# Local-and-global attention before a feed-forward layer: the softmax laid out by quarters of 32 queries with their global keys in the same 128 columns

## The chip, the cores and the metric

The kernel runs on one core of a Trainium2 chip. The metric is the time of one execution on the device in microseconds (us). The kernel before took 942.32 us, the median of 3 runs (941.04 to 943.88). TensorE is called PE here, VectorE DVE, ScalarE ACT, GpSimd POOL; SP is the engine whose queue issues nearly all transfers.

## The reference

```python
B, H, Sl, D = 8, 8, 512, 64;  Sg = 32;  window = 32;  scale = 1 / sqrt(D)
k_all, v_all = concat([k_g, k_l]), concat([v_g, v_l])         # along the keys
out_g = softmax(scale * q_g @ k_all.T) @ v_all                # 32 global queries see all 544 keys
s_ll  = where(abs(i - j) <= window, scale * q_l @ k_l.T, -1e9)  # local: a band of 65 keys
s_l   = concat([scale * q_l @ k_g.T, s_ll])                   # and the 32 global keys
out_l = softmax(s_l) @ v_all
x = concat([out_g, out_l], axis=2), heads side by side        # 4352 rows of 512
h = x @ w_in                                                  # 512 -> 2048
y = where(h > 0, h, exp(min(h, 0)) - 1) @ w_out               # 2048 -> 512
```

All inputs are fp32 but the two weight matrices, which are float64. The output is fp32.

## The kernel before

The program has two parts that run interleaved: attention, which makes x, and the feed-forward part, which takes x in blocks of 256 rows.

**Feed-forward.** The weights arrive as pairs of 32-bit words and are converted to a high and a low fp16 part (`unit`, on ACT, POOL and DVE). x is split in the same way (`split_x`). Each product is made of three fp16 matmuls (high x high, high x low, low x high). The first four blocks or so run in groups a to d as the weights become ready; later blocks run as group "f" and use a scheme of seven products of halves for the second matmul (`ffn2_seven`, line 488) in place of eight. `ffn1` is line 329, its activations lines 339 to 367. `add_up` (lines 280 to 295) prepares sums of weights for that scheme.

**Attention.** The work is cut into tiles (b, g, t): batch b of 8, group g of 4 heads, and t, a stretch of 128 of the 512 local queries; 64 tiles in all. Two heads lie in the two halves of the 128 partitions of a k or q tile (row half r), and j counts such pairs, so a group's four heads are (j, r). For each group `stage_ga` computes the scores of the 32 global queries against all keys (L714 for local keys, L717 for global ones) and the softmax of it; the normalised result is pg (local keys, L743) and pk (global keys, one 32x32 square per head, L742). Then per tile:

- scores (L775): each half of 64 queries meets 160 keys, namely its own 64, 32 on the left, 32 on the right and the 32 global ones (columns 128 to 159 of k, constant KW = 160). One matmul is 64 rows x 64 weight columns x 160 moving columns and uses a quarter of the array; four of them, (half, r), lie beside each other.
- softmax (L787 adds the mask and takes the maximum on DVE, L793 the exponential on ACT, L797 and L798 the reciprocal on DVE, L800 scales the 128 local columns on POOL, L802 the 32 global ones on DVE into pz).
- stage_t (L837) transposes the local part of each head; one copy (L839) puts it into ptw, a tile whose other halves are zero.
- stage_u transposes pz (L753), pg (L756) and for t = 0 also pk (L755), and copies them with three copies on ACT (L757, L759, L761) into ptw and ptg; L764 adds up pk's four squares.
- values: the global keys first (L881 in a single tile, with 128 rows of zero-padded values; L917 in a pair of tiles, with 32 rows, four heads in the four row groups of the array), then the local keys in two matmuls a head (L850, 128 rows x 64 weight columns x 96 moving columns: 64 local queries and the 32 global queries). The copies to x are L887 and L925.

Batches 0 and 1 go tile by tile (`stage_s`, `stage_v`): the scores of tile i, the transposes of tile i - 2 and the values of tile i - 3 in one slot (LAGT, LAGV). From batch 2 on, tiles go by pairs (`stage_ss`, `stage_vv`): both tiles' scores in one go on PE, later both tiles' transposes, later both tiles' values.

**What sets the order.** Attention is a generator whose steps are numbered; the table PACE says how many steps of the feed-forward part should be done by each attention step, and the loop at the end of `attn_ffn` advances the feed-forward part to that number. Steps 0 to 65 are the lead, in which the feed-forward part does not run yet (PACE's second entry). `defer(n, f)` puts a piece of work n steps later. The framework then orders the instructions of each engine by the program's order and its own planner's costs, and adds the waits. PSUM has pools of banks: ps_a with 4 banks (tile "pa": scores, transposes, values, and ffn1 of group "f"), ps_h and ps_o with 2 each. SP's queue issues transfers in its order; a transfer into a tile that is still read waits there, and what is behind it waits too. v has 3 buffers, vg 2, k and q 4 each.

The transfers of attention are k (640 KB for two heads of a batch), q (256 KB), v (256 KB a tile), qg and the global values: vg, 32 KB a group, or vpT, 128 KB a group, zero-padded, for batches 0 and 1.

Of the kernel before, what the change touches and what calls it, by code (L numbers as in the profile page):

```python
# [22 lines left out]
P = 128  # L23
NT = SL // P
HQ = P // 2
KW = HQ + 3 * 32
GW = P + 32
# [7 lines left out]
NPT = 3  # L35
# [26 lines left out]
def attn_ffn(ctx: ExitStack, tc: tile.TileContext, qT, qgT, kT, vT, vgT, vpT, w_in, w_out, mask, out):  # L62
# [44 lines left out]
    msk = wts.tile([P, 3, KW], F32, name="msk")  # L107
# [11 lines left out]
    for p in ptw[:2]:  # L119
        clear(p)  # L120
    pkd = [wts.tile([P, P], F32, name=f"pk{i}") for i in range(2)]
    pps = [wts.tile([P, 4, KW], F32, name=f"p{i}") for i in range(LAGT + 1)]
# [6 lines left out]
    for p in pkd:  # L129
        nc.gpsimd.memset(p, 0.0)  # L130
# [540 lines left out]
    def attention():  # L671
        np_ = [0]
        tiles = [0]
# [16 lines left out]
        def load_v(b, g, t):  # L690
            v = apool.tile([P, 8, D], F32, name="v", bufs=3)
            nc.sync.dma_start(v, vT[b, g, t])
            return v

        def load_vg(b, g):
            if b < PAIRED:
                i = (2 * b + g) % 3
                vg = ptw[2].rearrange("p a x -> p (a x)")[:, i * 4 * D:(i + 1) * 4 * D].rearrange("p (h d) -> p h d", h=4)
                nc.sync.dma_start(vg, vpT[b, g])
                return vg  # L700
            vg = apool.tile([P, D], F32, name="vg", bufs=2)
            nc.sync.dma_start(vg, vgT[b, g])
            return vg

        def stage_ga(st, g):
            halves = [ps_a.tile([P, 512], F32, name="pa") for _ in range(2)]
            qg = st["qg", g]
            for i in range(2):
                for j in range(2):
                    for r in range(2):  # L710
# [3 lines left out]
                        nc.tensor.matmul(halves[i][h, 0:NT * HQ], qg[rows, j, :], k[:, :, i, HQ * i:HQ * i + HQ],  # L714
                                         start=True, stop=True)
                        if i == 0:
                            nc.tensor.matmul(halves[0][h, NT * HQ:NT * HQ + 32], qg[rows, j, :], k[:, 0, 0, P:KW],  # L717
                                             start=True, stop=True)
            pg = apool.tile([P, NT, 2, HQ], F32, name="pg")
            pk = pkd[g]  # L720
            m = apool.tile([P, 4], F32, name="mg")
            s = apool.tile([P, 4], F32, name="sg")
            pu = apool.tile([P, 32], F32, name="pu", bufs=1)
            st["pg", g] = pg, pk
# [411 lines left out]
```

## Time and profile before

The profile is one execution of the program with the hardware profiler on.

| | |
|---|---|
| median of 3 runs | 942.32 us |
| the profiled execution | 944.38 us |
| its span, first to last instruction | 942.6 us |
| instructions | 23830 |
| mean granted TensorE clock | 0.981 |
| HBM read, written | 70.89 MB, 15.20 MB |
| lead (no feed-forward matmuls) | to about 76 us |

How to read the lines: a group of instructions has its source line (L775), engine, operation, the tile it writes and those it reads (out<-in), its shape (for PE rows * weight columns, then partitions x moving columns), how often it occurs, then busy time in us and the mean in ns of one, then the engine's idle time before it and what ended that. PEld are PE's weight loads. In the table by windows each row has a stretch of time, its length, then for each engine busy us with the count of instructions, the granted clock, the mean busy share of the 16 DMA engines and the GB/s moved. In the timeline the columns are start in us, duration in us, engine, line, operation and count. PE's matmuls overlap in its pipe, and their ends are modelled.

### The profile page before, as it was taken

What the parts mean: (1) busy time and instruction counts of PE and PEld (TensorE: products, weight loads), DVE (VectorE), ACT (ScalarE), POOL (GpSimd) and SP (SyncE); (2) the same over time, 40 slices, a digit from 0 to 9 for tenths busy, and PEclk for the clock granted to TensorE, in tenths of its full rate; (3) what the DMA queues carried; (4) which work ended last, traced back from release to release, by engine and by line L of the source; (5) the groups of instructions that cost most, each with busy time, mean ns of one, the idle gap of its engine ahead of it and who ended that gap; (6) DMA issues with size and microseconds to landing.
All of it is one profiled execution on the core that took longest, in us unless ns stands there. A gap on an engine that the chain in (4) does not pass through costs nothing.

```text
span 942.6 us, 23830 instructions
## 1 busy us (share of the span) xinstructions
PE 897.9 (95%) x9216; PEld 727.4 (77%) x9216; DVE 728.9 (77%) x2025; ACT 670.1 (71%) x1584; POOL 250.5 (27%) x483
## 2 busy tenths in 40 slices
PE   6889889799999999999999999999999999999997
PEld 3567555566666788888888888888888888888886
DVE  4988989899867867777776878686877777766566
ACT  5889998776667667676766767777867677666564
POOL 4665481540321222131132212212032112200000
PEclk7889999899999999999999999999999999999999
DMA  6855866232432124001320123002310101000000
GB/s 265 306 177 191 288 217 227 99 113 67 141 133 66 40 102 144 8 26 46 134 95 26 44 104 127 26 26 102 101 51 25 47 24 35 2 24 23 1 24 23
DMA packets 41769, 87.64 MB, mean 93 GB/s; under 512 B 7736, under 2 KB 8888, under 8 KB 41656
## 3 DMA queue, kind: packets, MB, share of 16 engines
q1 hardware_dynamic: 41368, 85.85, 26.8%
q8 instruction: 73, 1.20, 0.5%
q14 instruction: 40, 0.33, 0.1%
q10 hardware_dynamic: 288, 0.26, 0.1%
HBM read 70.89 MB, written 15.20 MB: 91 GB/s over the span
## 4 chain that ended last, share of the span: by engine, by line
PE 63%; DVE 19%; ACT 9%; POOL 5%; issue 3%; DVEq 0%; ACTq 0%; POOLq 0%
PE pa L329 24%; PE acc L488 11%; PE h L488 9%; PE h L329 4%; PE acc L453 3%; PE pa L850 2%; PE pa L775 2%; DVE gl L351 2%; ACT p L793 2%; PE pa L837 2%; POOL p L800 2%; DVE cu L280 2%; ACT gh L367 1%; DVE gx L348 1%; PE pa L714 1%
## 5 line engine op out<-in xcount | busy, mean ns | idle before, releaser
L329 PEld LDWEIGHTS <-winh 128*128 128x128 f16 x2160 | 210.6, 98 | 34.6 <-issue 3.1
L329 PE MATMUL pa<-xh,winh 128*128 128x256 f16 x824 | 224.8, 273 | 0.0
L329 PE MATMUL pa<-xl,winh 128*128 128x256 f16 x824 | 224.6, 273 | 0.0
L329 PE MATMUL pa<-xh,winl 128*128 128x256 f16 x824 | 224.6, 273 | 0.0
L800 POOL TENSOR_SCALAR p<-p,sm 128x128 f32<-128x128 f32 x256 | 127.3, 514 | 296.1 <-ACT p L793 190.2
L367 ACT ACTIVATE gh<-gx,xs 128x896 f16<-128x896 f32 x103 | 107.5, 1043 | 129.7 <-DVE gx L364 129.5
L351 DVE SCALAR_TENSOR_TENSOR gl<-gx,xs,gh 128x896 f16<-128x896 f32 x103 | 118.5, 1151 | 63.2 <-ACT gh L367 61.1
L488 PEld LDWEIGHTS <-gh 128*128 128x128 f16 x1456 | 140.2, 98 | 23.0 <-issue 7.6
L329 PEld LDWEIGHTS <-winl 128*128 128x128 f16 x1080 | 106.2, 98 | 14.7 <-issue 1.7
L793 ACT ACTIVATE p<-p,m 128x160 f32<-128x160 f32 x256 | 106.0, 416 | 6.0 <-DVE m L787 5.8
L339 ACT ACTIVATE g<-pa,xs 128x512 f32<-128x512 f32 x103 | 70.7, 686 | 22.4 <-PE pa L329 21.8
L341 ACT ACTIVATE g<-g 128x512 f32<-128x512 f32 x135 | 85.3, 632 | 0.1
L488 PE MATMUL acc<-wouth,gh 128*128 128x256 f16 x312 | 85.2, 273 | 0.0
L488 PE MATMUL acc<-wouth,gl 128*128 128x256 f16 x312 | 85.0, 273 | 0.0
L488 PE MATMUL acc<-woutl,gh 128*128 128x256 f16 x312 | 85.0, 273 | 0.0
L488 PEld LDWEIGHTS <-gl 128*128 128x128 f16 x728 | 71.2, 98 | 9.3 <-DVE gl L351 1.0
L488 PE MATMUL h<-raw,gh 128*128 128x256 f16 x416 | 74.2, 273 | 0.0
L329 PE MATMUL h<-xh,winh 128*128 128x256 f16 x256 | 71.2, 279 | 1.4 <-ACT hs L340 1.4
L329 PE MATMUL h<-xl,winh 128*128 128x256 f16 x256 | 71.1, 278 | 1.2 <-DVE xl L578 1.2
L329 PE MATMUL h<-xh,winl 128*128 128x256 f16 x256 | 71.1, 278 | 0.0
L348 DVE SCALAR_TENSOR_TENSOR gx<-g,p 128x512 f32<-128x512 f32 x52 | 36.2, 696 | 34.0 <-ACT g L341 32.8
L787 DVE CUSTOM_DVE_ANT_0 p<-pa,msk 128x160 f32<-128x160 f32 x228 | 60.7, 318 | 0.4 <-PE pa L775 0.4
(236 smaller groups left out, 2006.1 us busy)
## 6 DMA issues: line engine op xcount, KB each, us to landing
k<-kT SPq DMA_DIRECT2D x32, 640.0 KB, 5.1
v<-vT SPq DMA_DIRECT2D x64, 256.0 KB, 2.9
q<-qT SPq DMA_DIRECT2D x32, 256.0 KB, 5.6
raw<-w_in SPq DMA_DIRECT2D x8, 1024.0 KB, 5.8
raw<-w_out SPq DMA_DIRECT2D x8, 1024.0 KB, 5.6
out<-o SPq DMA_DIRECT2D x32, 256.0 KB, 2.1
od<-o SPq DMA_DIRECT2D x24, 256.0 KB, 2.2
o<-od SPq DMA_DIRECT2D x24, 256.0 KB, 2.8
```

Source lines behind the costliest of these rows:

```text
L280: nc.vector.tensor_add(w, wout[0][:, pr, :], wout[1][:, pr, :])
L329: nc.tensor.matmul(h[:, j, :], wt[:, c, f], xt[:, c, :], start=k == 0, stop=k == 11)
L339: nc.scalar.activation(g, hf, AF.Relu, scale=sc[:, p:p + 1])
L341: nc.scalar.activation(g, g, AF.Exp, scale=-1.0)
L348: nc.vector.scalar_tensor_tensor(out=out, in0=ins[0], scalar=-1.0, in1=ins[1], op0=ALU.add, op1=ALU.max)
L351: nc.vector.scalar_tensor_tensor(out=dst, in0=src, scalar=sg, in1=hi, op0=ALU.mult, op1=ALU.subtract)
L367: nc.scalar.activation(gh, gx, AF.Copy, scale=sg)
L453: nc.tensor.matmul(acc[t], gt[:, s], wt[:, f, :], start=p == first and j == 0 and k == 0, stop=p == last and j == 1 and k == 2)
L488: nc.tensor.matmul(cols, gt, w, start=p == 0 and k == 0, stop=last and k == len(todo) - 1, skip_group_check=True)
L787: nc.vector.tensor_tensor_reduce(out=ps[i], in0=places[divmod(i, 2)], in1=msk[:, mi, :], op0=ALU.add, op1=ALU.min, scale=-scale, scalar=3. ...
L793: nc.scalar.activation(ps[i], ps[i], AF.Exp, bias=m[:, i:i + 1], scale=-1.0, accum_out=s[:, 0, i:i + 1])
L800: nc.gpsimd.tensor_scalar(ps[i][:, 0:P], ps[i][:, 0:P], s[:, 1, i:i + 1], 1.0, ALU.mult, ALU.mult)
```

## The change

Softmax is laid out by quarters of 32 queries (w = 0 to 3). A quarter sees at most 96 local keys; with the 32 global keys these make 128 columns. The host lays out k so that the global keys stand inside each half's 160 columns (after the left 32 keys in the first half, before the right 32 in the second), and each quarter of a half takes a window of 128 of them. Hence:

- scores: per head and tile four matmuls of 64 rows x 32 weight columns x 128 moving columns in place of two of 64 x 64 x 160. For a pair of tiles, all scores lie in two PSUM banks in place of four.
- softmax on 128 columns in place of 160; POOL scales all 128 columns, and pz with L802 is gone.
- the global queries' softmax lies in one persistent tile pg of 800 columns (blocks of 96: 32 zeros and 64 keys; the global keys at the end), so that any 128 columns from a block's start match the keys of the second quarter of a half or the first quarter of the next; pk with its four scalings and L764 are gone.
- transposes: four of p and two of pg in every tile; one copy of 128x256 in stage_u in place of three. All of it lies in one tile pt of 192 columns a head with 2 buffers, in place of ptw and ptg with 3 (2 for batches 0 and 1).
- values: per head and tile four matmuls of 128 rows x 64 weight columns with 32, 64, 64 and 32 moving columns, which hold local and global keys together; the separate matmuls for the global keys (L881, L917) are gone.
- transfers: v holds values for four windows a head, 512 KB a tile in place of 256 KB; vg and vpT are gone.

The core of the diff:

```diff
-NPT = 3
+NPT = 2
...
-    ptw = [wts.tile([P, 2, 4 * (HQ + 32) + 32], F32, name=f"ptw{i}") for i in range(NPT)]
-    ptg = [wts.tile([P, PW], F32, name=f"ptg{i}") for i in range(NPT)]
-    def clear(p):
-        nc.gpsimd.memset(p[HQ:P, 0, :], 0.0)
-        nc.gpsimd.memset(p[0:HQ, 1, :], 0.0)
...
-    pkd = [wts.tile([P, P], F32, name=f"pk{i}") for i in range(2)]
-    pps = [wts.tile([P, 4, KW], F32, name=f"p{i}") for i in range(LAGT + 1)]
+    pgs = [wts.tile([P, 2 * NT * 96 + 32], F32, name=f"pg{i}") for i in range(2)]
+    pps = [wts.tile([P, 4, P], F32, name=f"p{i}") for i in range(LAGT + 1)]
...
-            v = apool.tile([P, 8, D], F32, name="v", bufs=3)
+            v = apool.tile([P, 16, D], F32, name="v", bufs=3)
...
-        def load_vg(b, g):
...
-                for h in range(4):
-                    q = slice(32 * h, 32 * h + 32)
-                    nc.gpsimd.tensor_scalar(pk[q, q], pu[q, :], s[q, 3:4], 1.0, ALU.mult, ALU.mult)
                 nc.gpsimd.tensor_scalar(pg, pg, s[:, 3:4], 1.0, ALU.mult, ALU.mult)
...
         def stage_u(st, g, t):
-            nc.tensor.transpose(tp[:, P:2 * P], st["pz", g, t].rearrange("p h x -> p (h x)"), ident)
-            if t == 0:
-                nc.tensor.transpose(tp[:, 2 * P:3 * P], pk, ident)
-            nc.tensor.transpose(tp[:, 0:P], pg[:, t].rearrange("p a x -> p (a x)"), ident)
-            (three nc.scalar.copy into pt and pz, and for t == 0 one nc.vector.tensor_reduce into pz)
+            for a in range(2):
+                o = 96 * (2 * t + a)
+                nc.tensor.transpose(tp[:, a * P:(a + 1) * P], st["pg", g][:, o:o + P], ident)
+            nc.scalar.copy(pt[:, :, HQ:2 * HQ].rearrange("p h (a q) -> p a h q", a=2),
+                           tp[:, 0:2 * P].rearrange("p (a h q) -> p a h q", a=2, h=4))

         def scores(st, g, t, places):
             for j in range(2):
-                for half in range(2):
+                for w in range(4):
                     for r in range(2):
                         rows = slice(64 * r, 64 * r + 64)
-                        qs = slice(t * P + half * HQ, t * P + (half + 1) * HQ)
-                        nc.tensor.matmul(places[j, r][half * HQ:(half + 1) * HQ, :], q[rows, qs], k[rows, t, half, :],
+                        qs = slice(t * P + 32 * w, t * P + 32 * w + 32)
+                        ks = slice(32 * (w % 2), 32 * (w % 2) + P)
+                        nc.tensor.matmul(places[j, r][32 * w:32 * w + 32, :], q[rows, qs], k[rows, t, w // 2, ks],
                                          start=True, stop=True)
...
-                    nc.gpsimd.tensor_scalar(ps[i][:, 0:P], ps[i][:, 0:P], s[:, 1, i:i + 1], 1.0, ALU.mult, ALU.mult)
-                pz = st["pz", g, t] = apool.tile([P, 4, 32], F32, name="pz")
-                nc.vector.tensor_tensor(out=pz, in0=pp[:, :, P:KW], in1=s[:, 1, :].unsqueeze(2).to_broadcast([P, 4, 32]),
-                                        op=ALU.mult)
+                    nc.gpsimd.tensor_scalar(ps[i], ps[i], s[:, 1, i:i + 1], 1.0, ALU.mult, ALU.mult)
...
         def stage_ss(st, g, t):
-            places = []
-            for x in range(2):
-                sp = [ps_a.tile([P, 512], F32, name="pa") for _ in range(2)]
-                places.append({(j, r): sp[r][:, j * KW:(j + 1) * KW] for j in range(2) for r in range(2)})
+            sp = [ps_a.tile([P, 512], F32, name="pa") for _ in range(2)]
+            places = [{(j, r): sp[r][:, (2 * x + j) * P:(2 * x + j + 1) * P] for j in range(2) for r in range(2)}
+                      for x in range(2)]
...
-        def local_v(o, st, g, t, h, i):
-            x = pt[:, 0, 32 + 96 * h:128 + 96 * h] if i == 0 else pt[:, 1, 96 * h:96 + 96 * h]
-            nc.tensor.matmul(o[:, HQ * i:HQ * i + 96], v[:, 4 * i + h, :], x, start=False, stop=i == 1, skip_group_check=True)
+        def values(o, st, g, t, h, w, start):
+            n, at, to = ((32, 0, 0), (64, 32, 32), (64, 96, 64), (32, 160, 128))[w]
+            nc.tensor.matmul(o[:, to:to + n], st["v", g, t][:, 4 * h + w, :], st["pt", g, t][:, h, at:at + n],
+                             start=start, stop=True, skip_group_check=True)
...
         def stage_vv(st, g, half):
-            for s in (1, 0):
-                for h in (2, 3, 0, 1):
-                    o, x = globals_x(out(s, h), st["pt", g, ts[s]][1][rows, :], ts[s])
-                    nc.tensor.matmul(o, vg[rows, :], x, start=s == 1, stop=False, skip_group_check=True)
-            (then local_v for s, j, i, r)
+            for j in (1, 0):
+                for s in range(2):
+                    for w in range(4):
                         for r in range(2):
-                            local_v(out(s, 2 * j + r), st, g, ts[s], 2 * j + r, i)
+                            values(banks[j][64 * r:64 * r + 64, s * PW:(s + 1) * PW], st, g, ts[s], 2 * j + r, w,
+                                   (s, w) == (0, 0))
```

`stage_ga` keeps its matmuls and exponentials, with columns taken from the new places. `stage_v` runs `values` over j, w and r in the same way. The order of stages, PACE, and the numbers of buffers of k, q and v are as before.

More of the change, by code (lines that the diff above doesn't have):

```diff
@@ L61, in attn_ffn @@
 @with_exitstack
-def attn_ffn(ctx: ExitStack, tc: tile.TileContext, qT, qgT, kT, vT, vgT, vpT, w_in, w_out, mask, out):
+def attn_ffn(ctx: ExitStack, tc: tile.TileContext, qT, qgT, kT, vT, w_in, w_out, mask, out):
     nc = tc.nc
@@ L875, in stage_v @@
             bank = v_bank()
[L876 removed]
             for j in range(2):
[L878 to L882 removed]
+                for w in range(4):
                     for r in range(2):
[L884 removed]
+                        values(bank[64 * r:64 * r + 64, j * PW:(j + 1) * PW], st, g, t, 2 * j + r, w, (j, w) == (0, 0))
             pv = bank[:, 0:2 * PW].rearrange("p (j a x) -> p j a x", j=2, a=2)
@@ L1100, in _layout @@
             o = t * P + half * HQ
-            own, left, right = range(o, o + HQ), range(o - 32, o), range(o + HQ, o + HQ + 32)
-            kT[:, :, :, t, half, P:KW] = k_g.transpose(0, 1, 3, 2)
-            for c, key in enumerate([*own, *left, *right] if half == 0 else [*left, *right, *own]):
-                if 0 <= key < SL:
-                    kT[:, :, :, t, half, c] = klT[..., key]
-                    vW[:, :, t, half, c] = v_l[:, :, key]
-                qs = np.arange(o, o + HQ)
-                seen = (abs(qs - key) <= 32) & (0 <= key < SL)
-                mask[half * HQ:(half + 1) * HQ, 0 if t == 0 else (2 if t == NT - 1 else 1), c] = np.where(seen, f(0), neg)
@@ L1110, in _layout @@
-    kT = kT.reshape(B, H // 2, P, NT, 2, KW)
-    vT = vW.reshape(B, 2, 4, NT, 2, P, D).transpose(0, 1, 3, 5, 4, 2, 6).reshape(B, 2, NT, P, 8, D)
-    vgT = v_g.reshape(B, 2, P, D)
-    vpT = np.zeros((PAIRED, 2, 4, 32, 4, D), f)
-    for h in range(4):
-        vpT[:, :, h, :, h] = v_g[:PAIRED].reshape(PAIRED, 2, 4, 32, D)[:, :, h]
-    vpT = vpT.reshape(PAIRED, 2, P, 4, D)
-    return dict(qT=qT, qgT=qgT, kT=kT, vT=vT, vgT=vgT, vpT=vpT, w_in=moe_w_in.view(np.int64), w_out=moe_w_out.view(np.int64), mask=mask)
+            near, shared = [*range(o - 32, o + HQ + 32)], [None] * 32
@@ new lines, in _layout @@
+            cut = 32 if half == 0 else 96
+            keys = near[:cut] + shared + near[cut:]
+            for c, key in enumerate(keys):
+                if key is None:
+                    kT[:, :, :, t, half, c] = k_g[:, :, c - cut]
+                elif 0 <= key < SL:
+                    kT[:, :, :, t, half, c] = klT[..., key]
+            for w in range(2):
+                qs = np.arange(o + 32 * w, o + 32 * w + 32)
+                rows = slice(half * HQ + 32 * w, half * HQ + 32 * w + 32)
+                for c, key in enumerate(keys[32 * w:32 * w + P]):
+                    if key is None:
+                        vW[:, :, t, 2 * half + w, c] = v_g[:, :, c - cut + 32 * w]
+                        continue
+                    if 0 <= key < SL:
+                        vW[:, :, t, 2 * half + w, c] = v_l[:, :, key]
+                    seen = (abs(qs - key) <= 32) & (0 <= key < SL)
+                    mask[rows, 0 if t == 0 else (2 if t == NT - 1 else 1), c] = np.where(seen, f(0), neg)
```

81 lines of the change are left out of this document (18 added, 63 removed).

## The prediction

> **What bounds the kernel now.** I read the page's busy shares and chain first, then the table of busy time by windows, because the program has stages with different limits.
>
> ```profile
> PE 897.9 (95%) x9216; PEld 727.4 (77%) x9216; DVE 728.9 (77%) x2025; ACT 670.1 (71%) x1584; POOL 250.5 (27%) x483
> ...
> PE 63%; DVE 19%; ACT 9%; POOL 5%; issue 3%; DVEq 0%; ACTq 0%; POOLq 0%
> ```
>
> ```profile
> core 0: us, PE busy (x) PEld busy (x) DVE busy (x) ACT busy (x) POOL busy (x), PEclk, DMA share, GB/s
> 507.05:509.12 2.07, 2.07 (x50) 1.78 (x49) 1.61 (x4) 0.39 (x1) 0.00 (x0) 1.00 0.07 16
> 498.82:500.07 1.25, 1.25 (x34) 1.02 (x33) 1.22 (x4) 0.00 (x0) 0.00 (x0) 1.00 0.00 0
> 5.00:76.00 71.00, 56.06 (x627) 37.88 (x626) 57.42 (x252) 54.11 (x182) 43.45 (x87) 0.83 0.69 243
> 76.00:240.00 164.00, 147.75 (x1245) 99.93 (x1244) 148.88 (x341) 133.16 (x283) 69.36 (x106) 0.98 0.52 174
> 240.00:800.00 560.00, 553.95 (x6067) 466.78 (x6066) 429.09 (x1242) 398.18 (x991) 128.67 (x270) 1.00 0.21 69
> ```
>
> From 240 to 800 us PE is idle for 6 us of 560, at full clock, while DVE, ACT and the DMA engines have room: there a microsecond off PE's own stream is a microsecond off the end. Before 240 us no engine is full: DVE is busy 81% and then 91%, PE 79% and 90%, and the chain runs through PE, DVE, ACT and POOL by turns. The two short windows are one value stage and one scoring stage of a pair of tiles; the timeline of PE shows what stands in them.
>
> ```profile
> 498.82 1.32 PE L775 MATMUL pa<-k,q 64*64 64x160 f32 x32
> 500.07 0.28 PE L488 MATMUL acc<-wouth,gh 128*128 128x256 f16 x1
> ...
> 507.05 0.67 PE L917 MATMUL pa<-ptg,vg 32*64 32x128 f32 x16
> 507.65 1.54 PE L850 MATMUL pa<-ptw,v 128*64 128x96 f32 x32
> 509.12 0.28 PE L329 MATMUL pa<-xh,winh 128*128 128x256 f16 x1
> ```
>
> An fp32 matmul of the code is two records. What one record costs while others follow it is not its listed mean (that holds the pipe's depth); the difference between two widths of one form is.
>
> ```profile
> L714 PE MATMUL pa<-k,qg 64*32 64x256 f32 x256 | 20.0, 388 | 3.1 <-DVE xg L930 3.1
> L717 PE MATMUL pa<-k,qg 64*32 64x32 f32 x128 | 4.4, 192 | 0.0
> ```
>
> ```profile
> L850 PEld LDWEIGHTS pa<-ptw,v 128*64 128x64 f32 x864 | 37.5, 137 | 4.8 <-issue 4.5 <-DMA q<-qT 0.2
> L714 PEld LDWEIGHTS pa<-k,qg 64*32 64x32 f32 x256 | 5.9, 108 | 8.0 <-DVE xg L930 3.3 <-issue 2.7 <-ACT ptw L839 0.4
> ```
>
> Streaming: (388 - 192) / 224 = 0.875 ns a column and record, so 28, 56, 84, 112 and 140 ns for 32, 64, 96, 128 and 160 columns. Loading weights: (137 - 108) / 32 = 0.91 ns a weight column, so 58 ns for 64. The stages agree. Scoring: 32 records over 4 subarrays are 8 rounds of 140 = 1.12 us, and 0.13 is left of 1.25 for entering and leaving the array mode. Values at L850: 32 records over 2 subarrays are 16 rounds of 84 = 1.34 of 1.47 us, again 0.13 left.
>
> **The change part by part, PE first.** How often each stage falls into the PE-bound window is counted by the window table for L917 (16 records a stage), L775 (32 a stage) and L753 (one a tile), in this order:
>
> ```profile
> 240.00:800.00 560.00, 15.23 (x352) 9.34 (x352) 1.00 0.21 69
> ...
> 240.00:800.00 560.00, 27.67 (x672) 21.46 (x672) 1.00 0.21 69
> ...
> 240.00:800.00 560.00, 12.22 (x44) 6.20 (x44) 1.00 0.21 69
> ```
>
> These are 22 value stages, 21 scoring stages and 44 tiles.
>
> *Scores.* 64 records of 128 columns in place of 32 of 160, over eight 64x32 subarrays in place of four 64x64: 8 rounds of 112 = 0.90 against 1.12 us, 0.22 saved a stage, 21 x 0.22 = 4.7 us. This needs eight streams at once, four of them from one row half; L714 shows four subarrays 64x32 together, two per half. Between 8 and 16 rounds I take 8.
>
> *Values.* The global stage L917 (0.60 us from 507.05 to 507.65, its mode change included) goes. The local stage becomes 64 records of 32 or 64 columns with 64-column weights each. Streaming alone would be 16 x (28 + 56 + 56 + 28) / 2 = 1.34 us, as before. But a load of 58 ns covers no 28 ns matmul: each of the 32 rounds costs the load, 1.86 + 0.13 = 1.99 us against 2.07. Stages with t = 0 save 0.06 more, since their two rounds of 160 columns at L917 go. Mean saving 0.11, 22 stages: 2.4 us. The bounds are 1.47 us a stage (loads hidden after all: 13.8 us saved) and 2.75 (supply, below). I take the load, since no row shows a matmul shorter than its own load. [...]
>
> *Transposes.* Per tile two and four remain; the transpose of pk for t = 0 goes. Transposes follow each other at 0.11 us:
>
> ```profile
> 495.56 0.27 PE L753 MATMUL pa<-ident,pz 128*128 128x128 f32 x1
> 495.67 0.27 PE L756 MATMUL pa<-ident,pg 128*128 128x128 f32 x1
> 495.78 0.27 PE L329 MATMUL pa<-xh,winh 128*128 128x256 f16 x1
> ```
>
> Of the 16 groups 10 fall after 240 us (two groups in each of batches 3 to 7): 10 x 0.11 = 1.1 us. Together 4.7 + 2.4 + 1.1 = 8.2 us in the PE-bound window.
>
> *The other engines.* Their rows:
>
> ```profile
> L787 DVE CUSTOM_DVE_ANT_0 p<-pa,msk 128x160 f32<-128x160 f32 x228 | 60.7, 318 | 0.4 <-PE pa L775 0.4
> L363 DVE TENSOR_TENSOR gx<-gx 128x256 f32<-128x256 f32 x103 | 44.7, 434 | 0.0
> L364 DVE TENSOR_TENSOR gx<-gx 128x128 f32<-128x128 f32 x103 | 30.5, 296 | 0.0
> L802 DVE TENSOR_TENSOR pz<-p,sm 128x128 f32<-128x128 f32 x64 | 21.4, 338 | 1.2
> L764 DVE TENSOR_REDUCE ptg<-pa 128x32 f32<-128x128 f32 x16 | 4.5, 283 | 0.2 <-ACT ptg L761 0.2
> ```
>
> ```profile
> L761 ACT COPY ptg<-pa 128x128 f32<-128x128 f32 x64 | 17.0, 265 | 0.9
> L759 ACT COPY ptw<-pa 64x128 f32<-64x128 f32 x64 | 16.7, 260 | 0.9
> L757 ACT COPY ptw<-pa 64x128 f32<-64x128 f32 x64 | 16.3, 254 | 8.9 <-PE pa L756 8.5
> L925 ACT COPY xr<-pa 128x256 f32<-128x256 f32 x48 | 15.2, 364 | 1.4 <-PE pa L850 1.4
> ```
>
> ```profile
> L742 POOL TENSOR_SCALAR pk<-pu,sg 32x32 f32<-32x32 f32 x64 | 33.1, 517 | 89.5 <-DVE sg L739 67.0 <-ACT hs L340 9.1 <-ACT p L793 9.0
> L743 POOL TENSOR_SCALAR pg<-pg,sg 128x512 f32<-128x512 f32 x16 | 13.9, 867 | 1.5
> ```
>
> DVE loses L802 (338 ns a tile) and 32 columns in each of four L787 (138/128 = 1.08 ns a column, 35 each): 0.48 us a tile, and L764 once a group. ACT trades three copies (779 ns) for one of L925's form (364), 0.42 us a tile, beside a little at the exponentials. POOL loses four L742 a group (2.07 us), while pg grows from 512 to 800 columns (at most 867 x 800/512, +0.49 us). After 240 us PE's stream covers all this: worth nothing. Before 240 us stand 64 - 44 = 20 tiles and 6 groups: 20 x 0.48 + 6 x 0.28 = 11 us of DVE. DVE shares the chain there with others, so I count a third: 3.5 us, between none and 11.
>
> *Transfers.* v doubles, the vg and vpT loads go.
>
> ```profile
> v<-vT SPq DMA_DIRECT2D x64, 256.0 KB, 2.9
> ...
> vg<-vgT SPq DMA_DIRECT2D x12, 32.0 KB, 3.6
> ```
>
> The first stage moves 243 GB/s at a share of 0.69, so 352 GB/s when full: 256 KB more are 0.74 us, and some 15 loads fall there: 11 us out of 22 idle ones. SP issues in order, so the k, q and weight loads behind a v land later by that. After 240 us v has a whole pair's time (from 500 to 507 us and longer) to land, at a share of 0.21. I charge nothing, and name the loss as a rival.
>
> *Waits.* Two buffers for pt instead of three of ptw: the copy into one waits for the matmuls that read it two tiles ago, which PE issued ahead of the transposes that this copy needs anyway, so nobody waits longer. Both score tiles of a pair share two PSUM banks instead of four: DVE's first L787 may have to start after all 64 matmuls, at most half a stage (0.45 us) later, with the exponentials two steps behind it; PE gets two banks more for the next h. Zeroing pg happens once, ahead of the first tile.
>
> **The sum.** The profiled execution took 944.4 us (span 942.6): 944.4 - 8.2 - 3.5 = 932.7. It lies 2.1 us above the median of the runs, 942.3, so the forecast there is 930.6 us.
>
> **The rivals**, on the median's scale.
>
> A. *Four streams from one row half don't run together.* Scoring then needs 16 rounds: 1.79 + 0.13 = 1.92 us, 0.67 more than now: 21 x 0.67 = 14.1 lost for 4.7 gained, 949 us, and about 3 more from the 16 single tiles: 952. It decides once a scoring stage takes over 1.58 us: 21 x 0.33 eats the other 2.4 + 1.1 + 3.5. Against it: L714 keeps all four column groups busy.
>
> B. *PE can't be fed with that many short instructions.* The densest long stretch is the value stage, 48 records in 2.07 us, 43 ns each. At 43 ns, 64 records take 2.75 us: scoring loses 21 x 1.50 = 31.5, values 22 x 0.68 = 15: 930.6 + 46.5 + 7.1 = 984. The new scoring stage needs 16 ns a record, the values 31. No row shows either rate for so long; but streaming alone already explains 43, so it is no sign of a limit. [...]
>
> C. *The early stage loses.* About six of its v loads stand ahead of something that is waited for: 6 x 0.74 = 4.5 us lost in place of 3.5 gained: 930.6 + 8.0 = 938.6. For it: the share of 0.69 and one queue. Against it: the one wait of PE on a transfer that the groups show is 1.0 us.
>
> ```profile
> L775 PE MATMUL acc<-k,q 64*64 64x160 f32 x112 | 8.4, 318 | 1.6 <-DMA q<-qT 1.0 <-DVE m L787 0.5
> ```
>
> D. *Loads hide under matmuls.* The value stage is then bound by streaming, 13.8 us saved for 2.4: 930.6 - 11.4 = 919. For it: the load and the matmul of other rows overlap without a gap. Against it: there the matmul is the longer of the two.
>
> **Chances.** Forecast (925 to 935) 0.58, C 0.14, D 0.11, A 0.08, B 0.05, and 0.04 for an order of instructions that the planner makes worse by more than is won. The range that leaves out at most 2 in 10 reaches from 918 (D) to 945 (C with its own width); A and B lie outside. Differences below 0.3% (939.5 to 945.1) can't be told from none here: 0.07, mostly of C. Slower is A, B and the planner, with a little of C: 0.16. Faster: 0.77.
>
> **What would show it.** L775's successor: 2048 records 64*32 with 128 columns, a paired stage of 1.03 us (A: 1.9; B: 2.75). L917's and L881's successors gone, value records 2048 of 128*64, half with 32 and half with 64 columns, a stage of 1.99 us (1.5 in D). From 240 us on PE's idle time stays near 6 us and that stretch is about 8 us shorter; the FFN's first block and the end of the conversion come some 3.5 us earlier (later in C, with waits on k, q or raw behind v). The forecast falls if the late stretch gains less than 4 us, or if the early one loses.

## The result and the profile after

The kernel after takes 935.63 us, the median of 4 runs (934.68 to 938.14), beside 943.1 us for the kernel before on the same chip (941.04 to 944.25): a ratio of 0.9927, 95% interval 0.99 to 0.9955. On a second chip it was 0.992 (0.9894 to 0.9946). So it is faster, by 7 to 7.5 us or 0.7 to 0.8%; 930.6 us (a gain of 11.7) had been forecast, with 918 to 945 as the range and 0.58 for 925 to 935. The profiled execution took 934.68 us, its span is 932.9.

All line numbers have moved: the scores are L741 now (L775 before), the values L803 (L850, L881 and L917), p's transposes L797 (L837), pg's L728 (L753, L755, L756), the mask and maximum L753 (L787), ffn1 L319 (L329), and the second matmul's L478 (L488). First the page's busy times and its chain, then the table by windows for all work, and then for the lines of scores, values and pg's transposes alone (their columns: PE busy with records, PEld busy, clock, DMA share, GB/s):

```profile
PE 888.6 (95%) x10736; PEld 723.2 (78%) x10736; DVE 702.0 (75%) x1945; ACT 637.1 (68%) x1456; POOL 206.2 (22%) x413
...
PE 50%; DVE 22%; ACT 18%; DMA 5%; issue 3%; POOL 2%; SPq 0%; DVEq 0%; ACTq 0%; POOLq 0%
```

```profile
5.00:76.00 71.00, 56.56 (x919) 36.35 (x918) 53.59 (x238) 48.44 (x167) 36.78 (x70) 0.81 0.76 278
490.73:491.82 1.09, 1.09 (x65) 0.89 (x65) 1.06 (x4) 0.00 (x0) 0.00 (x0) 1.00 0.00 0
498.80:500.79 1.99, 1.99 (x65) 1.95 (x65) 1.32 (x3) 0.98 (x3) 0.93 (x3) 1.00 0.03 8
...
240.00:800.00 560.00, 24.29 (x1344) 18.66 (x1344) 1.00 0.25 88
...
240.00:800.00 560.00, 47.35 (x1472) 44.79 (x1472) 1.00 0.25 88
...
240.00:800.00 560.00, 16.79 (x88) 11.04 (x88) 1.00 0.25 88
```

PE is as full as before, with 1,520 more records. The short windows are one paired scoring stage and one paired value stage: 1.09 us, where 1.25 stood, and 1.99 us, where 2.07 stood. The last three rows count 21 scoring stages (1344 / 64), 23 value stages (1472 / 64) and 44 tiles after 240 us; the value stages are 23 in the kernel before as well when they are counted by their start. PE's timeline shows what stands in the two:

```profile
490.73 1.16 PE L741 MATMUL pa<-k,q 64*32 64x128 f32 x64
491.82 0.28 PE L478 MATMUL acc<-wouth,gh 128*128 128x256 f16 x1
...
498.80 2.06 PE L803 MATMUL pa<-pt,v 128*64 128x32 f32 x64
500.79 0.28 PE L319 MATMUL pa<-xh,winh 128*128 128x256 f16 x1
```

Where the time went is read best at a mark that both traces have: the scoring stage of tiles 20 and 21, the first one after 200 us. Soon after it PE is full. The two stages, before and then after:

```profile
235.23 1.32 PE L775 MATMUL pa<-k,q 64*64 64x160 f32 x32
```

```profile
234.06 1.16 PE L741 MATMUL pa<-k,q 64*32 64x128 f32 x64
```

From this mark to the end of the span it is 942.6 - 235.2 = 707.4 us before and 932.9 - 234.1 = 698.8 after: 8.6 us of gain late, 1.1 early. But these two executions differ in the clock too. The next paired stage, the scores of tiles 22 and 23, cuts the late part in two; the rows are from tile 20 to tile 22 and from there to the end, for the kernel before, for the kernel before with a fill in its lead alone (e7 below), and for the kernel after:

```profile
235.23:263.02 27.79, 25.75 (x229) 18.10 (x228) 24.50 (x58) 18.17 (x46) 10.70 (x12) 0.94 0.39 124
263.02:942.60 679.58, 669.26 (x7172) 573.93 (x7171) 502.52 (x1385) 468.67 (x1083) 124.33 (x267) 1.00 0.17 56
```

```profile
239.80:265.98 26.18, 24.15 (x229) 17.27 (x228) 24.49 (x58) 18.19 (x46) 10.71 (x12) 1.00 0.36 131
265.98:945.50 679.52, 669.26 (x7172) 573.98 (x7171) 502.28 (x1385) 469.01 (x1083) 124.36 (x267) 1.00 0.16 56
```

```profile
234.06:259.86 25.80, 24.29 (x277) 17.30 (x276) 23.87 (x56) 15.51 (x39) 8.66 (x12) 1.00 0.45 154
259.86:932.90 673.04, 662.63 (x8186) 573.07 (x8185) 483.09 (x1333) 446.73 (x999) 95.13 (x227) 1.00 0.21 72
```

From tile 22 on the gain is 6.5 us, and PE's busy time falls by about that, 6.6. Between the marks the profiled execution of the kernel before was granted half the clock for 3.4 us (the 0.94 of the first row), which made the same work 1.6 us longer than in e7. So the late part of the kernel before at full clock is 705.7 us, its gain is 6.9, and the 1.6 us more in the two profiles are the clock's and not the change's. The late part of the kernel after is 698.8 us also in its second profile and in that of the first experiment below. The medians gained 7.5 us on the one chip and 7.2 on the other, which leaves 0.3 to 0.6 us for the early part if the median executions had the full clock late; by the far ends of the two intervals it is 2.5 and 3.1 at most. Of the 3.5 us that were forecast there, little is to be seen.

### The profile page after: what moved, and what is told of

Read it like the earlier page. It is cut to its first block, busy times and chain, and to the rows that moved or that the text cites. A ratio compares the mean times of both kernels' runs of the same rounds, so it can differ in the third digit from the quotient of the medians.

```text
span 932.9 us, 26318 instructions
## 1 busy us (share of the span) xinstructions
PE 888.6 (95%) x10736; PEld 723.2 (78%) x10736; DVE 702.0 (75%) x1945; ACT 637.1 (68%) x1456; POOL 206.2 (22%) x413
## 4 chain that ended last, share of the span: by engine, by line
PE 50%; DVE 22%; ACT 18%; DMA 5%; issue 3%; POOL 2%; SPq 0%; DVEq 0%; ACTq 0%; POOLq 0%
PE pa L319 19%; PE acc L478 9%; PE h L478 7%; ACT p L759 5%; DVE gl L341 4%; ACT gh L357 3%; DVE gx L338 3%; PE acc L443 3%; PE pa L803 3%; PE h L319 2%; DMA raw<-w_out 2%; PE pa L797 2%; DMA od<-o 2%; ACT g L329 2%; ACT g L331 2%
## 5 line engine op out<-in xcount | busy, mean ns | idle before, releaser
L319 PEld LDWEIGHTS <-winh 128*128 128x128 f16 x2160 | 209.7, 98 | 36.3 <-issue 6.6
L319 PE MATMUL pa<-xh,winh 128*128 128x256 f16 x824 | 224.9, 273 | 0.8 <-DVE xglob L873 0.8
L319 PE MATMUL pa<-xl,winh 128*128 128x256 f16 x824 | 224.7, 273 | 0.0
L319 PE MATMUL pa<-xh,winl 128*128 128x256 f16 x824 | 224.7, 273 | 0.0
L766 POOL TENSOR_SCALAR p<-p,sm 128x128 f32<-128x128 f32 x256 | 117.5, 477 | 328.8 <-DVE sm L764 297.7
L341 DVE SCALAR_TENSOR_TENSOR gl<-gx,xs,gh 128x896 f16<-128x896 f32 x103 | 122.5, 1189 | 75.4 <-ACT gh L357 75.4
L478 PEld LDWEIGHTS <-gh 128*128 128x128 f16 x1456 | 140.1, 98 | 22.6 <-issue 7.0
L319 PEld LDWEIGHTS <-winl 128*128 128x128 f16 x1080 | 106.0, 98 | 16.5 <-issue 3.7
L759 ACT ACTIVATE p<-p,m 128x128 f32<-128x128 f32 x256 | 99.3, 390 | 25.8 <-DVE m L753 25.7
L478 PE MATMUL acc<-wouth,gh 128*128 128x256 f16 x312 | 85.3, 273 | 0.0
L478 PE MATMUL acc<-wouth,gl 128*128 128x256 f16 x312 | 85.1, 273 | 0.0
L478 PE MATMUL acc<-woutl,gh 128*128 128x256 f16 x312 | 85.1, 273 | 0.0
L478 PEld LDWEIGHTS <-gl 128*128 128x128 f16 x728 | 71.2, 98 | 9.3 <-DVE gl L341 1.0
L329 ACT ACTIVATE g<-pa,xs 128x512 f32<-128x512 f32 x103 | 70.2, 681 | 9.7 <-PE pa L319 9.1
L478 PE MATMUL h<-raw,gh 128*128 128x256 f16 x416 | 74.3, 273 | 0.0
L319 PE MATMUL h<-xl,winh 128*128 128x256 f16 x256 | 70.7, 277 | 3.3 <-DVE xl L568 3.3
L319 PE MATMUL h<-xh,winh 128*128 128x256 f16 x256 | 70.6, 277 | 3.2 <-ACT hs L330 2.1
L319 PE MATMUL h<-xh,winl 128*128 128x256 f16 x256 | 70.7, 277 | 0.0
L803 PEld LDWEIGHTS pa<-pt,v 128*64 128x64 f32 x1728 | 53.3, 139 | 8.0 <-issue 6.3
```

Of the source, the lines that this page charges most:

```text
L319: nc.tensor.matmul(h[:, j, :], wt[:, c, f], xt[:, c, :], start=k == 0, stop=k == 11)
L329: nc.scalar.activation(g, hf, AF.Relu, scale=sc[:, p:p + 1])
L341: nc.vector.scalar_tensor_tensor(out=dst, in0=src, scalar=sg, in1=hi, op0=ALU.mult, op1=ALU.subtract)
L478: nc.tensor.matmul(cols, gt, w, start=p == 0 and k == 0, stop=last and k == len(todo) - 1, skip_group_check=True)
L759: nc.scalar.activation(ps[i], ps[i], AF.Exp, bias=m[:, i:i + 1], scale=-1.0, accum_out=s[:, 0, i:i + 1])
L766: nc.gpsimd.tensor_scalar(ps[i], ps[i], s[:, 1, i:i + 1], 1.0, ALU.mult, ALU.mult)
```

## The experiments

In the table the early part is the start of tile 20's scores in the median run (its start in the profile, plus the median, less the profiled execution's time; for the kernel before with the 705.7 us of e2 and e7 as its late part); the late part is from there to the span's end in the profile. The ratio is to the kernel before on the same chip; e1 to e4 ran on one chip, e5 to e8 on a second, e9, e10 and e12 on a third, e11 on a fourth, where the kernel before took 944.1, 944.3, 945.5 and 943.9 us, so across chips the ratios compare better than the times.

| kernel | tile 20, profile | late part | median | early part, median run | ratio (95%) |
|---|---|---|---|---|---|
| before | 235.2 | 707.4 | 943.1 to 945.5 | 235.6 to 238.0 | 1 |
| after | 234.1 | 698.8 | 935.63 | 235.0 | 0.9927 (0.99 to 0.9955) |
| after, second chip (e5) | 234.2 | 698.8 | 937.09 | 236.6 | 0.992 (0.9894 to 0.9946) |
| e1: v 256 KB | 240.1 | 698.8 | 936.51 | 235.9 | 0.9916 (0.9889 to 0.9944) |
| e2: before, v copied once more | 248.7 | 705.7 | 958.84 | 251.3 | 1.0158 (1.0122 to 1.0195) |
| e3: scores in 64x64 | 236.4 | 697.4 | 937.11 | 237.9 | 0.9922 (0.9897 to 0.9948) |
| e4: a unit more in the lead | 233.9 | 696.7 | 934.53 | 236.1 | 0.9905 (0.9876 to 0.9933) |
| e6: PE fill in the lead | 243.7 | 699.3 | 941.45 | 240.4 | 0.9963 (0.9945 to 0.9981) |
| e7: before with that fill | 239.8 | 705.7 | 946.94 | 239.4 | 1.0021 (1.0005 to 1.0038) |
| e8: e4 and e6 together | 237.0 | 696.8 | 935.82 | 237.2 | 0.9902 (0.9879 to 0.9926) |
| e9: DVE work added | 237.2 | 699.3 | 938.56 | 237.5 | 0.9937 (0.9913 to 0.996) |
| e10: ACT work added | 246.6 | 700.2 | 944.5 | 242.5 | 1.0009 (0.9988 to 1.0029) |
| e11: e1 and e4 together | 235.7 | 696.8 | 933.4 | 234.8 | 0.9888 (0.9863 to 0.9914) |
| e12: two units more | 236.9 | 698.5 | 936.07 | 235.8 | 0.99 (0.9879 to 0.992) |

The granted clock isn't the same in all kernels. Its mean over all executions is 0.979 to 0.980 in the kernel before on each of the four chips, and 0.978 and 0.979 in the kernel after (the first run and e5). It is 0.974 to 0.975 in e1, e2, e4 and e12, 0.972 to 0.973 in e3, e9, e10 and e11, 0.981 in e6, 0.985 in e7 and 0.979 in e8. Among the executions of one kernel 0.001 of it goes with about 0.5 us (156 executions, each against the mean of its kernel and chip). So of two kernels that lie 0.005 apart, some 2 to 3 us may go with the clock. Whether an edit lowers the clock or something else does isn't shown, since the kernel after itself ran in the first run and beside e6 to e8 alone. The early parts below are to be read with that reservation.

**Are v's bytes what ate the early gain?** e1 loads half of v (the rest of the values comes from wrong blocks); e2 adds as many bytes again to the kernel before, as a copy into memory that nobody reads.

```diff
 e1, on the kernel after
-            v = apool.tile([P, 16, D], F32, name="v", bufs=3)
+            v = apool.tile([P, 8, D], F32, name="v", bufs=3)
...
-            nc.tensor.matmul(o[:, to:to + n], st["v", g, t][:, 4 * h + w, :], st["pt", g, t][:, h, at:at + n],
+            nc.tensor.matmul(o[:, to:to + n], st["v", g, t][:, (4 * h + w) % 8, :], st["pt", g, t][:, h, at:at + n],
 e2, on the kernel before
+            nc.sync.dma_start(dram.tile([P, 8, D], F32, name=f"again{b}{g}{t}"), vT[b, g, t])
```

> The changed kernel with v of 8 blocks (256 KB a tile, as in the kernel before) in place of 16; the values' matmuls keep their number and shapes but take block (4h + w) mod 8, so the values are wrong. Only the bytes of v differ. The lead of the changed kernel ends 3.6 us earlier than before (first feed-forward matmul at 71.9 us against 75.5), yet its feed-forward matmul number 300 starts 0.6 us later than before (143.3 against 142.7). Theory T (v's doubled bytes delay the weights' and the od transfers between 76 and 175 us): here number 300 starts at 139.5 us or earlier, number 750 at about 228 (230.7 in the changed kernel), transfers leave the chain of waits, and the time is 2 to 4 us below the changed kernel's 935.6, so about 932. Rival P (the conversion of the weights, paced by steps and by its own engines, gives the lead's gain back whatever v costs): number 300 stays within 1 us of 143 and the time within 1 us of 935.6. After 240 us both expect no difference.

> The kernel before with each v loaded a second time, 256 KB more a tile, into a place in DRAM that nobody reads (so with 16 MB of extra writes too). Theory T: the lead and the conversion are late, feed-forward matmul number 300 starts 2 to 5 us after 142.7 and the time is 2 to 5 us above 943. Rival P: within 1 us in both.

Measured: e1 936.51 us, within its interval the same as after, at a clock lower by 0.004; its 300th feed-forward matmul starts at 145.9 us, later and not earlier, in a profile that is the slowest of its six executions. e2 958.84, 14.8 us more than before on that chip, all of it ahead of tile 20 (its late part is 705.7). The traces show the mechanism of rival C at one place of the lead. PE's timelines have the scores of tile 8 in the three kernels (before, after, e1); the rows are the first scores that start between 46 and 61 us:

```profile
47.42 0.80 PE L775 MATMUL acc<-k,q 64*64 64x160 f32 x4
```

```profile
57.41 0.45 PE L741 MATMUL acc<-k,q 64*32 64x128 f32 x16
```

```profile
50.30 0.38 PE L741 MATMUL acc<-k,q 64*32 64x128 f32 x2
```

```profile
v<-vT SPq DMA_DIRECT2D x64, 512.0 KB, 4.6
...
raw<-w_out SPq DMA_DIRECT2D x8, 1024.0 KB, 7.0
```

Tile 8 starts 10 us later after the change, and 7 of the 10 come back in e1; the loads of v and w_out take 4.6 and 7.0 us to land, where 2.9 and 5.6 stood (2.9 and 5.3 in e1). But the attention catches up inside the lead: tile 12 starts at 70.4 us in the profile after, 70.7 in e1 and 72.9 before. (In the kernel after values that stand ahead of these scores in the other two come behind them; tile 13 starts at 77.4, 80.6 and 78.2 us.) So v's bytes do delay transfers, and giving them back shows no gain at the end; a gain of some 2 us could hide behind e1's lower clock. e2 shows that transfers can be the bound there (from 140 to 180 us the mean busy share of the DMA engines is 0.87, where 0.58 stood); it is no fair double of v, since it also writes 256 KB a tile and puts one more issue on SP's queue.

**Is the scoring stage held by the supply of instructions?** It was forecast at 1.03 us and takes 1.089. e3 uses the 64x64 arrays again, with 128 columns (the keys of a half's second quarter are left out, so the scores aren't the reference's): the same streaming of 8 rounds of 112 ns, with half the records.

```diff
-                for w in range(4):
+                for half in range(2):
...
-                        nc.tensor.matmul(places[j, r][32 * w:32 * w + 32, :], q[rows, qs], k[rows, t, w // 2, ks],
+                        nc.tensor.matmul(places[j, r][HQ * half:HQ * half + HQ, :], q[rows, qs], k[rows, t, half, 0:P],
```

> The changed kernel with the scores as 64 x 64 x 128 matmuls, two halves in place of four quarters: half as many instructions over four subarrays, the second quarter of each half gets the first one's keys, so the output is not the reference's. Rounds and streamed columns are those of the changed kernel. [...]

Its paired stage on PE's timeline:

```profile
492.31 1.10 PE L740 MATMUL pa<-k,q 64*64 64x128 f32 x32
493.35 0.28 PE L478 MATMUL acc<-wouth,gh 128*128 128x256 f16 x1
```

It is 1.04 us long (1.036 in all 21 of them), just the forecast's 1.03: the formula of rounds was right, and what came on top for 64 records is the rate at which they come; what sets that rate no run shows. In the stage after, the records start about 6.7 ns apart in groups of eight, 109 ns from group to group, until the 37th record; from there on, within a group, most follow at 16 to 17 ns, and the last one starts at 888 ns, where e3's last starts at 835. 21 x 0.053 = 1.1 us; e3's late part is shorter by 1.4. Its median is no better, since its early part came out 1 to 3 us longer, at the lowest clock of all (0.972).

**Does the conversion of the weights set the early part?** Its 16th unit's last step on DVE starts at the same time before and after (the rows of that line in the two kernels, with count, shortest, median and longest in ns, first and last start in us):

```profile
L221 DVE SCALAR_TENSOR_TENSOR woutl<-cu,cm,wouth x8: 1269/1277/1285, 28.8 to 192.3; 128x1024 f16<-128x1024 f32 x8
```

```profile
L211 DVE SCALAR_TENSOR_TENSOR woutl<-cu,cm,wouth x8: 1272/1281/1295, 29.9 to 192.0; 128x1024 f16<-128x1024 f32 x8
```

e4 allows one more unit to run in the lead, e12 two more; e11 is e4 with e1's small v.

```diff
-UNITS = 0, 1, 8, 18, 30
+UNITS = 0, 1, 8, 18, 30, 44           (e4, e8, e11)
+UNITS = 0, 1, 8, 18, 30, 40, 52       (e12)
```

> The changed kernel with one more conversion unit started in the lead, at attention step 44 (UNITS = 0, 1, 8, 18, 30, 44). Rival P, that the conversion's own pace sets the stretch from 76 to 175 us: number 300 starts 2 to 4 us earlier than 143.3 and the time falls by 2 to 3 us to about 933. Theory T, transfers: 1 MB more has to come in the lead, which is at a transfer share of 0.76; the lead gets 1 to 3 us longer and the time stays within 1.5 us of 935.6.

> The kernel after, with UNITS longer by two entries (40 and 52), that is, two more units of the weights' conversion are allowed to run in the lead. Theory U (the early part is set by how soon the conversion is through): the 300th feed-forward matmul starts by 139.8 us or sooner (143.3 in the kernel after; 139.8 with one more entry, 44), and the median is 934 us or less. Theory O (one more entry was already all that helps, or its gain was chance): 935 to 937 us, or above where the units delay the lead's attention.

> Two edits together on the kernel after: v with eight blocks a tile as in e1 (256 KB; the last heads meet values that are not theirs, so the output leaves the reference), and one more unit of the weights' conversion allowed in the lead as in e4. The traces of the other kernels show the conversion of the weights through at the same time before and after the change (its 16th and last low part starts at 192.3 and 189.3 us), though the lead had become 3.6 us shorter; in the kernel after, its sixth unit is taken up at 76.6 us, in e1 at 65.4, in e4 at 69.7. Theory P (the conversion's pace sets the time to about 230 us, and v's bytes slow it): the gains of e1's and e4's edits add up, the sixth unit starts by 66 us, the 300th feed-forward matmul by 138 us (143.3 after, 139.8 e4), the median is 932 us or less. Theory Q (the bytes cost nothing even then): as e4, the 300th matmul at about 140 us and a median of 934 to 936.

The lead's 3.6 us of that last text hold for the first feed-forward matmul alone, a lone piece; 12 matmuls later the kernel after is only 0.8 us ahead (76.0 against 76.8 us). And its 189.3 us is the last low part of w_in; that of w_out starts at 192.0 us, as shown above. Measured in e4 and in e11:

```profile
L211 DVE SCALAR_TENSOR_TENSOR woutl<-cu,cm,wouth x8: 1277/1281/1296, 30.0 to 181.6; 128x1024 f16<-128x1024 f32 x8
```

```profile
L211 DVE SCALAR_TENSOR_TENSOR woutl<-cu,cm,wouth x8: 1271/1278/1454, 30.4 to 181.7; 128x1024 f16<-128x1024 f32 x8
```

The conversion is through 10 us sooner, the 300th feed-forward matmul starts at 139.8 and 139.7 us instead of 143.3, and yet tile 20 comes at 236.1 and 234.8 us in the median run, as in the kernel after. So the conversion's pace alone doesn't set the early part to its end, as far as their lower clock lets one say; theory P's adding up of the two edits shows in the sixth unit (58.2 us, 66 expected) and not in the 300th matmul (138 expected); the median, 933.4, lies between P's 932 and Q's 934. What e4, e8 and e11 do have is a late part shorter by 2 us, and it is won between tile 20 and tile 22. The row of e4:

```profile
233.87:257.48 23.61, 23.61 (x278) 17.38 (x277) 19.17 (x48) 13.90 (x35) 5.63 (x12) 1.00 0.48 168
```

In the kernel after PE waits there for POOL (1.0 us) and ACT (0.5 us), and DVE is busy for 23.87 of 25.80 us; in e4 PE has no idle time, and DVE has 19.17 us of work. The feed-forward matmuls are the same, 768 ahead of tile 20 and 135 between the marks in both. What moved ahead is DVE's work, 48 instructions in place of 56. e12's two units bring no more (936.07 us, its 300th matmul at 147.8 us, later and not earlier): theory O. But e12 is no pure test. One more block goes by the seven products (L443's records fall from 384 to 288, L478's rise from 2184 to 2352), and its profiled execution had half the clock for 3.4 us at 269 us, which can explain why its late part is 1.8 us longer than e4's. The four ratios with longer UNITS (0.9888 to 0.9905) all lie below the two of the kernel after, but each interval overlaps those: some 2 us are likely and not shown. Among those that compute the reference e12 (0.99), e8 (0.9902) and e4 (0.9905) can't be told apart.

**Is it the clock, or PE's own work in the lead?** The granted clock from 5 to 76 us was 0.83 before and 0.81 after. e6 puts four idle fp16 matmuls of 512 columns into each of the 11 transposing steps of the lead, to keep PE busier; e7 does it to the kernel before, e8 to e4.

```diff
+            for _ in range(4 if lead[0] else 0):
+                nc.tensor.matmul(tp, warm[:, 0:P], warm, start=True, stop=True)
```

> The changed kernel once more, beside the others of this call. Its ratio to the kernel before should again be 0.993 (0.990 to 0.9955).

> The changed kernel with four idle fp16 matmuls of 128x512 (weights and moving data are zeros) into the bank of stage_t ahead of its transposes, in the lead alone; the result is the same. In the profiles so far the granted clock falls to one half for stretches of 3 to 17 us in the first 105 us: 30.8 us of them in the changed kernel, 24.0 in the kernel before, and executions of one kernel differ by about 0.7 us of span for each 0.001 of mean clock. Theory K (the early gain was lost because PE, with less to do, is granted half the clock for longer, and the lead waits for PE at half speed): the half-clock time before 105 us falls below 20 us, feed-forward matmul number 300 starts 2 us or more earlier and the time falls by 2 to 4 us against the changed kernel. Rival P (the conversion's own pace, clock of no account): number 300 and the time stay within 1 us, or the time rises by up to 2 us, as 16 x 4 x 0.21 = 14 us of matmuls come into the lead.

> The kernel before with the same four idle matmuls in stage_t in the lead. Theory K: its half-clock time before 105 us (24.0 us) falls less than the changed kernel's, and the time falls by 0 to 2 us. Rival P: unchanged within 1 us, or slower by up to 2 us.

> The changed kernel with both: the conversion unit at attention step 44 and the four idle matmuls. If both the conversion's pace and the clock take part, the gains add up: 2 us from the unit and 2 to 4 from the clock, a time 4 to 6 us below the changed kernel's. If only the pace counts, it equals the run with the unit alone (ratio 0.9905).

e6's first row by windows:

```profile
5.00:76.00 71.00, 59.97 (x952) 37.21 (x951) 52.84 (x236) 48.14 (x163) 37.27 (x69) 0.86 0.77 278
```

The kernel after once more (e5) took 937.09 us. With the fill (e6) the clock of that window rose to 0.86, and the kernel became 4.4 us slower than that; the kernel before became 2.6 slower (e7). That doesn't yet decide theory K, since the fill did little for the clock as a whole: in the profiles the half-clock time before 105 us fell from 30.0 us to 23.9, not below 20, and up to 240 us it is 41.0 in e6 and 37.5 in the kernel after. What speaks against K is that the kernels before and after have the same mean clock on e5's chip (0.979 each, over 23 and 6 executions). 44 matmuls of 512 columns are by estimate about 9.7 us of PE at full clock (0.22 us each, twice the 0.11 us at which L319's matmuls of 256 columns follow each other in the kernel after), and a quarter to a half of it is paid (more, if e7's higher clock gave something back): PE's own work counts in the lead, though PE is idle for a fifth of that time. With e4's unit more the fill costs nothing that can be seen (e8's ratio is 0.9902, e4's 0.9905).

**What is a microsecond of DVE or of ACT worth there?** e9 gives DVE two operations like pz's in each tile's softmax, e10 gives ACT two copies in each stage_u; nobody reads their results.

```diff
 e9
+                for _ in range(2):
+                    nc.vector.tensor_tensor(out=apool.tile([P, 4, 32], F32, name="pz"), in0=msk[:, 0, :].rearrange("p (h x) -> p h x", h=4),
+                                            in1=s[:, 1, :].unsqueeze(2).to_broadcast([P, 4, 32]), op=ALU.mult)
 e10
+            for a in range(2):
+                nc.scalar.copy(apool.tile([P, P], F32, name="pz"), tp[:, a * P:(a + 1) * P])
```

> The kernel after, with two more operations of pz's kind on DVE in every tile's softmax (a multiplication of 128x128 elements, 338 ns each in the profile before; their results are read by nobody): 0.68 us a tile, 13.5 us of DVE over the 20 tiles ahead of 240 us, somewhat more than the 11 us that the change took off DVE there. Theory R (the early relief of DVE was worth a third of itself, and something else in the change ate it): the first 240 us become longer by about 4.5 us, the median goes to about 940 us. Theory N (the early relief is worth nothing, because DVE's work there is covered by the conversion's other engines and by PE's own queue): the start of the 750th feed-forward matmul stays within 1 us of 230.7 us, and the median within 1 us of the kernel after (936 to 937). From 240 us on both expect no more than 1 us, since DVE is idle a quarter of that stretch.

> The kernel after, with two more copies on ACT in every tile's stage_u (128x128 each, about 265 ns by L761 of the profile before; their results are read by nobody): 0.53 us a tile, 10.6 us of ACT over the 20 tiles ahead of 240 us, about what the change took off ACT there (0.42 us a tile). The prediction gave ACT's relief no worth. Theory N (no engine but PE counts): within 1 us of the kernel after, 936 to 937. Theory R' (ACT's relief is what the early part gained): a third of it is lost, 3.5 us in the first 240 us, median about 940.

The added operations, in the groups of e9 and e10, and e10's first two windows:

```profile
L768 DVE TENSOR_TENSOR pz<-msk,sm 128x128 f32<-128x128 f32 x128 | 33.9, 306 | 1.2
```

```profile
L732 ACT COPY pz<-pa 128x128 f32<-128x128 f32 x128 | 29.0, 289 | 0.0
```

```profile
5.00:76.00 71.00, 51.24 (x817) 33.78 (x825) 48.51 (x211) 47.15 (x161) 33.53 (x61) 0.76 0.70 252
76.00:240.00 164.00, 142.64 (x1422) 95.88 (x1408) 140.37 (x335) 129.62 (x290) 67.52 (x104) 0.95 0.57 191
```

Ahead of tile 20 stand 40 of each: 12.2 us of DVE (40 x 0.306) and 11.6 of ACT (40 x 0.289). By the ratios, e9 is slower than the kernel after by 0.9 to 1.6 us (0.0010 to 0.0017 of 945), of which 0.5 lie in the late part: DVE's 12.2 us cost about 1 us early, or up to 2.5 by the medians. The intervals of the two ratios leave some 3 us either way, and e9's clock was lower by some 0.005. By the signs that were set neither theory holds: the 750th feed-forward matmul starts at 233.8 us, 3 us later and not within 1, and the median lies between N's 937 and R's 940. So DVE's price lies somewhere between nothing and R's third. e10 is slower by 7.7 to 8.4 us (0.0082 to 0.0089), 1.4 of it late: ACT's 11.6 us cost some 6 to 7 us early, more than half of it, though ACT is busy for 48 us of 71 in the first stage of the kernel after. Part of that may go with e10's lower clock. What the clock doesn't touch is the step from e9 to e10, on one chip at 0.973 and 0.972: 5.9 us, of which 0.9 are late, so ACT's added work costs some 5 us more than DVE's. In e10's profile tile 12's scores start at 76.7 us instead of 70.4, so most of that is lost in the lead. Theory N falls for ACT; R' had the sign right, and its 3.5 us look too small. Whether ACT's time itself or the longer hold of the PSUM bank that the copies read makes the price was not separated.

## Why the prediction was right and where it was wrong

The sign, the mechanism of the late part and the range held. The size was 5 us too good. 935.6 lies just outside the 925 to 935 that the forecast was given, and by the number alone it is nearer to rival C's 938.6. Of the 5 us some 1.3 are the late part's, 2.9 the early part's, and 0.8 come in because the kernel before took 943.1 us beside it and not 942.3. The terms say where:

| term | forecast | measured |
|---|---|---|
| scores, 21 paired stages | 0.22 each, 4.7 us | 1.250 to 1.089 us, 0.161 each, 3.4 us |
| values, paired stages | 2.07 to 1.99, 2.4 us | 48.18 to 45.80 us for 23 stages, 2.4 us |
| transposes | 1.1 us | L728's stage 0.218 us, 0.328 before where t = 0: 1.1 us |
| late part | 8.2 us | 6.9 by these terms, and 6.9 between the late parts at full clock (705.7 and 698.8) |
| early part | 3.5 us | 0.3 to 0.6 for the medians, 1.1 between the profiles |

- *Scores.* Eight arrays of 64x32 do run together (8 rounds, 109 ns from one to the next, and not 16), which refutes rival A. The missing 0.06 us a stage (1.3 us in all) is what rival B named, at a price far below the one it was given: no limit at 43 ns a record, but a spacing of 16 to 17 ns after some 36 records. The forecast's "densest" stretch wasn't even the densest: the scoring stage before has 32 records in 1.25 us, 39 ns each. The "16 ns a record" that the prediction says this stage needs lies just at it.
- *Values.* The forecast's step was exact: a round is set by the load of 64 weight columns. In the stage after, the first records of its 32 rounds are spread over 1,829 ns, 59 ns each, while a 32-column matmul streams in 28 by L714's two widths, and PEld is busy for 1.95 of the 1.99 us. Rival D (loads hidden, 1.5 us) is out.
- *Early part.* This is the step that failed: "I count a third: 3.5 us". Its sign, that the conversion's end comes some 3.5 us earlier, isn't there either (192.0 against 192.3 us). e9 prices added DVE time there at about 1 us in 12; if a relief is worth as much, the 11 us were worth about 1 us and not 3.5, which is within what was measured. What stays unexplained is the other side. By e10 and e6 the 0.42 us of ACT a tile, which the prediction gave no worth, and PE's shorter single-tile stages should have gained something, and it isn't there. v's later landing (tile 8, 10 us late) is a loss, but e1 returns it without any gain that shows. Adding to an engine and relieving it need not have the same price: it may be that once one of the four is relieved, the others and the transfers still hold the tile, which no run tested. Why ACT's relief brought nothing stays open. The clock took no more after than before, by its means on e5's chip. The pace of the conversion is not shown to be the cause (e4 and e11 end it 10 us sooner, and tile 20 comes no earlier), nor are v's bytes (e1), though with the lower clock of these runs some 2 to 3 us can't be excluded for either.
- *Rival C.* Its mechanism is there (the w_out load 7.0 us to landing, tile 8 late), its price of 4.5 us is not: with v at 256 KB the median is the same, and e1's lower clock leaves room for some 2 us.
- *Nothing charged for waits.* From 240 to 800 us PE is idle for 5.6 us (560 - 554.40 in the row below) where it was 6.05, so two buffers for pt and two banks for a pair's scores cost nothing there.

```profile
240.00:800.00 560.00, 554.40 (x7208) 473.20 (x7207) 414.42 (x1210) 379.81 (x911) 98.17 (x232) 1.00 0.25 88
```

## What to carry to other kernels

In a stretch where one engine is full, count the rounds of each stage and price a round by the longer of its stream and its weight load; such a sum came out within 0.06 us a stage here. In a stretch where no engine is full, a relieved engine is not worth a guessed share: what added work costs on each engine can be measured (little on DVE here, a quarter to a half of its time on PE, about half on ACT), and even that does not say what a relief brings. Compare the granted clock of the runs first: two profiles of one stretch differed by 1.6 us through it alone. Halving the matmul's size to fill more of the array brought 0.161 us a scoring stage here, 0.06 less than its rounds promised, with the records 16 to 17 ns apart in the stage's second half.

## What the runs showed of the hardware

- In the kernel after's scoring stage of 64 records on 64x32 arrays (490.73 us) the records within a group of eight start about 6.7 ns apart up to the 37th; after that most come at 16 to 17 ns.
- Eight fp32 streams, four of them from the same 64 rows, run at once there: a round of 128 columns starts every 109 ns (the second 135 after the first), where L714's two widths give 112 for one stream.
- In the kernel after's value stage (498.80 us) the loads of 64 weight columns were not hidden by the shorter matmuls of their own kind: 59 ns a round on average, with 28 or 56 ns of streaming, and PEld busy for 1.95 of 1.99 us.
- Most of the spread lies ahead of tile 20: one and the same late part of 698.8 us stands in profiles (after and e1) whose executions took 934.7 and 940.7 us.
- In these profiles the granted clock falls to one half for stretches of 3.4 to 17.1 us. One of 3.4 us, in the kernel before at 252 us, made the same work take 27.8 us instead of 26.2.
